# State products of units 1 to 3 in the accumulators' banks, and two loads of unit 1 moved

## The chip, the cores and the metric

The kernel runs on one core of one Trainium2 chip. A core has a matrix engine (TensorE, "PE" in the profile), a vector engine (VectorE, DVE), an engine for pointwise functions (ScalarE, ACT), a general-purpose engine (GpSimd, POOL) and an engine that only issues transfers (Sync, SP). They run side by side, each takes its own instructions in order, and they wait for each other through semaphores. Matrix results are written to PSUM[...]; everything else lies in SBUF. Transfers from and to the main memory (DMA) can be issued by Sync, ScalarE and GpSimd.

The metric is the device time of one execution in microseconds, lower is better. Before the change it is 333.74 us, the median of three executions (333.68 to 335.12).

## What is computed

The reference has two parts. The first is a chunked state-space scan over `x`, with decay `a` and the vectors `B` and `C`:

```
log_a = log(clip(a, 1e-6, 1));  state = 0
for each chunk of 32 positions:
    cum  = cumsum(log_a in the chunk)
    M    = (C B^T) * exp(cum_i - cum_j), for j <= i
    y    = M x + (C state) * exp(cum)
    state = exp(sum(log_a)) * state + sum_j exp(cum_last - cum_j) * B_j x_j
```

with batch 4, 8 heads, 768 positions, head size 32 and state size 16. The second part takes the 3072 rows of `y`, 256 wide, through two dense layers: `out = silu(y @ w_in) @ w_out`, with a middle width of 2048.

## The kernel before

The positions are cut into twelve units of 256 positions (`UT`), three to a batch entry (`UPB`), and each unit into four chunks of 64. Units 0, 1 and 2 are the first batch entry, unit 3 starts the second. Two units make a block of 512 rows for the dense layers; units 0 and 1, whose dense layers run first and piece by piece, are the "first pass", which the change lies in and just ahead of.

Nothing here is scheduled by a tool: each engine runs its instructions in the order in which the program text issues them. What sets the order are the calls at the end of the kernel (from line 696), then the strings of `steps` (line 835), then `PLAN` (line 849) for the later blocks.

One unit goes through these helpers, named in the profile by their lines:

- `load_n`, `load_t`, `load_x` (L125, L135, L143) load B, C and x. `load_n(u, 0, q)` loads B and `load_n(u, 1, q)` loads C with positions on the partitions, in two transfers each, on the queue `q`. One run of B or C is 16 floats, 64 bytes; one run of x is 32 floats.
- `f_P0` (L344) clamps `a` for the prefix products and `f_P` (L348) scans them on DVE.
- `f_Ab` (L363) spreads `a` over the partitions by a matmul into a bank of the pool `ps_a`; `f_Ek` (L356) scans it on DVE into the decay matrix E.
- `f_B` (L380) multiplies B by the last column of E, giving BT, on GpSimd for units 1 and 2.
- `f_TP` (L394) transposes B and C on PE for units 0 to 2, and ACT copies them out (L398, L401); `f_T2` (L408) makes the head-masked copies of C.
- `f_G` (L442) forms C B^T on PE, into columns 0 to 255 of the four banks of a tile `gy`.
- `f_D0` (L428) forms the state products, BT times x, on PE. Before the change they go to columns 256 to 383 of the first two banks of the same tile `gy`.
- `f_M` (L448) multiplies E in place by the result of `f_G`, on DVE, in two halves. `f_S` (L460, L462) runs the state recurrence over the four state products, on DVE. `f_SM` (L469) makes masked copies of the states on ACT. `f_C` (L412) multiplies C by the prefix products.
- `f_Y` (L482, L491) adds up the state part and the in-chunk part of y on PE into a new tile `gy`, and `f_X` (L501) copies it out on ACT as the dense layers' input.

PSUM is divided into `gy` (`ps_s`, one buffer of four banks), `hp` (`ps_h`, two buffers of one bank) and `a` (`ps_a`, two buffers of one bank). The last pair holds the output sums of the second dense layer, from the first call of `f_s2` on (L544, at 60 us); before that it holds the spread `a` of units 0 and 1.

The weights come as raw 64-bit numbers, in sixteen tiles of 128 x 4 KB (`raw 0` to `raw 15`, L183), and are turned into 32-bit floats on the chip: `w_size` takes two ACT instructions (L189 and L192), `w_bits` three on DVE (L203, L205, L206) and an addition on GpSimd or DVE (L208). The first dense layer of the first pass is `f_s1` (L531), two per unit and weight tile. Matmuls on a tile of zeros, `busy` (L298, L300), fill places where PE would stand still.

Around the change, in the order of the program: ACT does `w_size(0, "u")`, then `f_SM(0)`, later `w_size(2)`, `f_SM(1)`, `w_size(3, "u")`, `f_X(1)`. DVE does `f_M(1, 0)`, `f_P(1)`, `f_M(1, 1)`, `f_S(1)`. PE does `f_s1(0, 0)`, `f_G(1)`, `f_s1(0, 1)`, `f_D0(1)`, six matmuls of zeros, `f_Y(1)`, and then `f_s1(1, 0)`. Sync's queue issues, after the store of `a` for the first batch entry (L259): x of unit 1, raw 2, ab 2 (L113), pa 2 (L246), acl (L265), raw 3, C and B of unit 2, raw 4, x of unit 2. GpSimd, once its masks are made, issues B of unit 1, clamps `a` for unit 0, issues C of unit 1, and then runs `f_C(0)`.

Of the kernel before, what the change touches and what calls it, by code (L numbers as in the profile page):

```python
# [33 lines left out]
def kernel(  # L34
# [22 lines left out]
    nc = tc.nc  # L57
# [5 lines left out]
    UPB = S // UT  # L63
# [22 lines left out]
    def block(name, dtype=FP32):  # L86

        return blk.tile([128, 512], dtype, name=name, tag="blk", bufs=NB)
# [4 lines left out]
    def bank4(name="gy"):  # L93
        return ps_s.tile([128, 4, 512], FP32, name=name, tag="gy")

    def acc(name):
        return ps_a.tile([128, 512], FP32, name=name, tag="a")
# [3 lines left out]
    def at(u):  # L101
        return u // UPB, u % UPB * UT
# [13 lines left out]
    def load_n(u, i, q, ks=(0, 1)):  # L116
        b, t0 = at(u)
        if i == 1:
            if u not in tbc:
                tbc[u] = block("tbc0")[:, 0:256].rearrange("p (k h n) -> p k h n", k=2, h=H)  # L120
        elif u not in bn:
            bn[u] = (block("bn0")[:, 0:256].rearrange("p (k h n) -> p k h n", k=2, h=H) if u in (0, 1, 3) else
                     loads.tile([128, 2, H, N], FP32, name="bn"))
        for k in ks:
            q.dma_start(out=(bn, tbc)[i][u][:, k], in_=(B, C)[i][b, :, t0 + 128 * k:t0 + 128 * k + 128].rearrange("h p n -> p h n"))  # L125
# [12 lines left out]
    def load_x(u, q, ks=(0, 1)):  # L138
        b, t0 = at(u)
        if u not in xt:  # L140
            xt[u] = loads.tile([128, 2, H, D], FP32, name="xt", bufs=2)
        for k in ks:
            q.dma_start(out=xt[u][:, k], in_=x[b, :, t0 + 128 * k:t0 + 128 * k + 128].rearrange("h p d -> p h d"))  # L143
# [28 lines left out]
    def two(t):  # L172
        return t.rearrange("p (k f) -> p k f", k=2)
# [82 lines left out]
    def f_A():  # L256
        nc.vector.tensor_scalar(out=ach[A0:A1], in0=ach[A0:A1], scalar1=1.0, scalar2=1e-6, op0=ALU.min, op1=ALU.max)
        nc.vector.memset(ach[A0:A1, :, 0:1], 0.0)
        nc.sync.dma_start(out=a_first, in_=ach[A0:A1])  # L259
# [30 lines left out]
    def early(n):  # L290
        t = half("zero")
        for i in range(n):
            nc.tensor.matmul(out=t, lhsT=warm[:, 0:128], rhs=warm, start=True, stop=True)
# [24 lines left out]
    nc.scalar.activation(misc[:, 2 * UT - 1:], idle[:, 0:1], AF.Silu)  # L318
    early(6)
    f_A()  # L320
    load_x(1, nc.sync)
    hm = const.tile([128, H], FP32, name="hm")
    nc.gpsimd.memset(hm, 1.0)
# [17 lines left out]
    def f_P0(u, engine):  # L341
        src = pa[u].rearrange("p (c t) -> p c t", t=Q)
        PZ[u] = (pz, pz1, pz)[u]
        engine.tensor_scalar(out=PZ[u][:, :, 1:], in0=src, scalar1=1.0, scalar2=1e-6, op0=ALU.min, op1=ALU.max)  # L344
# [16 lines left out]
    def f_Ab(u, k, hs=slice(0, H), bank=acc):  # L361
        t = ab[u, k, hs.start] = bank("ab").rearrange("p (h t) -> p h t", t=Q)
        nc.tensor.matmul(out=t[:, hs].rearrange("p h t -> p (h t)"),  # L363
                         lhsT=sel[:A1, 2 * u + k].rearrange("r c m -> r (c m)"),
                         rhs=ach[:A1, hs].rearrange("r h t -> r (h t)"), start=True, stop=True)
# [49 lines left out]
    def new_dp(u):  # L415
        if u not in DP:
            DP[u] = bank4()
        return DP[u]

    def f_D0(u, ts=(0, 1, 2, 3)):  # L420
        last = u % UPB == UPB - 1
        bt = BT[u].rearrange("p k h n -> p k (h n)")
        xc = xt[u].rearrange("p k h d -> p k (h d)")
        d = [new_dp(u)[:, c, 256:384].rearrange("p (k x) -> p k x", k=2) for c in range(2)]
        for t in ts[:3 if last else 4]:
            k, c = divmod(t, 2)
            for g in range(4):
                nc.tensor.matmul(out=d[c][32 * g:32 * g + 32, k],  # L428
                                 lhsT=bt[64 * c:64 * c + 64, k, 32 * g:32 * g + 32],
                                 rhs=xc[64 * c:64 * c + 64, k, 64 * g:64 * g + 64], start=True, stop=True,  # L430
                                 tile_position=(64 * c, 32 * g), skip_group_check=True)
        BX[u] = d
        if 3 in ts:
            BT.pop(u)
# [258 lines left out]
                in_=r[32 * q:32 * q + 32].rearrange("p (b d) -> p b d", d=32))  # L693


    load_n(1, 0, nc.gpsimd)
    f_P0(0, nc.gpsimd)
    load_n(1, 1, nc.gpsimd)
    f_Ab(0, 0, slice(0, 4))
    f_Ab(0, 0, slice(4, 8))  # L700
    f_Ab(0, 1, slice(0, 4), half)
# [18 lines left out]
    f_Ek(0, 1, slice(4, 8))  # L720
    f_B(0)
    f_D0(0)
    f_Ab(1, 0)
    f_Ab(1, 1)
# [26 lines left out]
    f_G(1)  # L751
    f_s1(0, 1)
    f_D0(1)
    f_M(1, 0)
    f_P(1)
# [20 lines left out]
    def stage(u, what):  # L776
        for c in what:
# [16 lines left out]
            elif c == "P":  # L794
                f_P(u)
            elif c in "12":
                f_E1(u, int(c) - 1, 2)
            elif c == "B":
                f_B(u, nc.gpsimd if u == 2 else nc.vector)
            elif c == "C":  # L800
                f_C(u)
            elif c == "D":
                f_G(u)
                f_D0(u)
            elif c == "M":
                f_M(u, 0)
                f_M(u, 1)
            elif c == "S":
                f_S(u)
            elif c == "s":  # L810
                f_SM(u)
            elif c == "Y":
                f_Y(u)
                f_X(u)
            elif c == "h":
                f_xh(u)
            elif c == "l":
                f_xl(u)
            elif c == "d":
                f_xd(u)  # L820
# [137 lines left out]
```

## Time and profile before

| | us |
|---|---|
| median of three executions | 333.74 |
| the profiled execution | 336.35 |
| its span, first to last instruction | 334.3 |
| PE busy in the span | 325.1 (97%) |
| DVE busy | 250.8 (75%) |
| ACT busy | 220.9 (66%) |
| GpSimd busy | 78.3 (23%) |
| first pass ends, about (first L544) | 60 |

The profile is of one execution, whose time is 2.6 us above the median; its span leaves 2.05 us outside. The page cuts the span into 40 slices of 8.4 us and gives the busy share of each in tenths:

```profile
PE   8888999999999999999999999999999999999996
PEclk9897999999999999999999999999999999999999
DMA  6897895796883684164420164520263000012001
```

A 9 is 90% or more. PE has room in the first four slices only, 0 to 33 us, and in the second and fourth its granted clock (PEclk) is not full. A matmul's end in the profile is modelled, so a busy PE is not one at its peak; and an engine's idle time counts only where the end of the kernel waits for it. A line of the waits reads: engine and line that waited, what it waited for, total time, times, longest. A line of the timeline reads: start, length, engine, line, operation, output from input, count, and in brackets the idle time before it with what ended it.

### The profile page before, as it was taken

What the parts mean: (1) busy time and instruction counts of PE and PEld (TensorE: products, weight loads), DVE (VectorE), ACT (ScalarE), POOL (GpSimd) and SP (SyncE); (2) the same over time, 40 slices, a digit from 0 to 9 for tenths busy, and PEclk for the clock granted to TensorE, in tenths of its full rate; (3) what the DMA queues carried; (4) which work ended last, traced back from release to release, by engine and by line L of the source; (5) the groups of instructions that cost most, each with busy time, mean ns of one, the idle gap of its engine ahead of it and who ended that gap; (6) DMA issues with size and microseconds to landing.
All of it is one profiled execution on the core that took longest, in us unless ns stands there. A gap on an engine that the chain in (4) does not pass through costs nothing.

```text
span 334.3 us, 7996 instructions
## 1 busy us (share of the span) xinstructions
PE 325.1 (97%) x3229; PEld 262.9 (79%) x3229; DVE 250.8 (75%) x414; ACT 220.9 (66%) x422; POOL 78.3 (23%) x81
## 2 busy tenths in 40 slices
PE   8888999999999999999999999999999999999996
PEld 4456888888878778778778778778778778899996
DVE  7769787896887988997965996965996873494443
ACT  3443876976577898766666666767666756656662
POOL 8332313687111222231202231202230202000000
PEclk9897999999999999999999999999999999999999
DMA  6897895796883684164420164520263000012001
GB/s 129 227 187 194 215 286 202 181 197 126 153 164 68 114 156 80 47 112 77 96 54 0 47 112 87 108 33 0 52 108 65 2 2 0 0 23 43 2 0 63
DMA packets 90709, 31.87 MB, mean 95 GB/s; under 512 B 74433, under 2 KB 81345, under 8 KB 90673
## 3 DMA queue, kind: packets, MB, share of 16 engines
q1 hardware_dynamic: 85296, 25.47, 34.2%
q0 software_dynamic: 3008, 5.51, 9.2%
q10 hardware_dynamic: 2368, 0.39, 0.6%
q8 instruction: 25, 0.41, 0.5%
q14 instruction: 12, 0.09, 0.1%
HBM read 22.79 MB, written 3.32 MB: 78 GB/s over the span
## 4 chain that ended last, share of the span: by engine, by line
PE 95%; DMA 1%; SPq 1%; DVE 1%; issue 1%; ACT 0%; DVEq 0%
PE hp L567 23%; PE hp L559 11%; PE hp L531 9%; PE oa L608 9%; PE oa L609 9%; PE b L639 9%; PE oa L544 8%; PE gy L491 3%; PE b L634 2%; PE b L617 2%; PE oa L617 2%; PE gy L482 2%; PE gy L442 2%; PE gy L428 1%; DMA xt<-in_x_dram 1%
## 5 line engine op out<-in xcount | busy, mean ns | idle before, releaser
L561 ACT ACTIVATE hp<-hp 128x512 f32<-128x512 f32 x80 | 46.6, 582 | 72.5 <-PE hp L559 72.4
L581 DVE TENSOR_TENSOR gl<-g,gh 128x512 fp32r<-128x512 f32 x62 | 42.7, 689 | 50.7 <-ACT gh L577 47.6
L567 PE MATMUL hp<-xh,wh 128*128 128x512 f32 x160 | 65.5, 409 | 0.0
L585 DVE SCALAR_TENSOR_TENSOR gd<-gh,g 128x512 fp32r<-128x512 f32 x80 | 59.5, 747 | 5.2 <-ACT gh L577 5.2
L567 PE MATMUL hp<-xl,wl 128*128 128x512 f32 x160 | 62.8, 393 | 0.0
L581 POOL TENSOR_TENSOR gl<-g,gh 128x512 fp32r<-128x512 f32 x18 | 29.2, 1622 | 122.1 <-ACT gh L577 122.1
L577 ACT ACTIVATE gh<-g 128x512 fp32r<-128x512 f32 x80 | 50.5, 632 | 2.8
L608 PE MATMUL oa<-gh,wh 128*128 128x512 f32 x128 | 50.1, 391 | 0.0
L609 PE MATMUL oa<-gl,wl 128*128 128x512 f32 x128 | 50.0, 391 | 0.0
L559 PE MATMUL hp<-xd,wd 128*128 128x512 f32 x160 | 49.6, 391 | 0.0
L575 ACT ACTIVATE g<-hp 128x512 f32<-128x512 f32 x80 | 47.4, 593 | 0.6 <-PE hp L567 0.6
L567 PEld LDWEIGHTS hp<-xh,wh 128*128 128x128 f32 x160 | 30.1, 188 | 8.8 <-ACT hp L561 2.5
L559 PEld LDWEIGHTS hp<-xd,wd 128*128 128x128 f32 x160 | 30.0, 188 | 6.8
L639 PE MATMUL b<-gd,wd 128*128 128x512 f32 x128 | 34.6, 390 | 0.0
L567 PEld LDWEIGHTS hp<-xl,wl 128*128 128x128 f32 x160 | 30.1, 188 | 4.8
L531 PE MATMUL hp<-xf,w 128*128 128x256 f32 x128 | 31.7, 403 | 0.5 <-ACT xf L501 0.5
L356 DVE TENSOR_TENSOR_SCAN E<-ab,diag 128x512 f32<-128x512 f32 (+1 forms) x26 | 29.4, 1165 | 1.6 <-PE gy L491 1.0
L531 PEld LDWEIGHTS hp<-xf,w 128*128 128x128 f32 x128 | 25.2, 202 | 4.7 <-ACT xf L501 0.6
L544 PE MATMUL oa<-gT,w 128*128 128x256 f32 x128 | 28.4, 379 | 0.0
L608 PEld LDWEIGHTS oa<-gh,wh 128*128 128x128 f32 x128 | 24.0, 188 | 5.2
L639 PEld LDWEIGHTS b<-gd,wd 128*128 128x128 f32 x128 | 24.0, 188 | 5.1
L609 PEld LDWEIGHTS oa<-gl,wl 128*128 128x128 f32 x128 | 24.0, 188 | 5.1
(104 smaller groups left out, 463.2 us busy)
## 6 DMA issues: line engine op xcount, KB each, us to landing
ab<-a_zero SPq DMA_DIRECT2D x18, 256.0 KB
raw<-in_moe_w_in_dram SPq DMA_DIRECT2D x8, 512.0 KB
raw<-in_moe_w_out_dram SPq DMA_DIRECT2D x8, 512.0 KB
wl<-w POOLq DMA_DIRECT2D x16, 256.0 KB, 4.2
xt<-in_x_dram SPq DMA_DIRECT2D x24, 128.0 KB
out_dram<-ot SPq DMA_DIRECT2D x40, 64.0 KB
tbc<-in_C_dram SPq DMA_DIRECT2D x40, 32.0 KB
bn<-in_B_dram SPq DMA_DIRECT2D x20, 64.0 KB
```

Of the source, the lines that this page charges most:

```text
L531: nc.tensor.matmul(out=hp[:, i], lhsT=two(w32[j])[:, kc, 128 * i:128 * i + 128], rhs=two(XF[u])[:, kc], start=(kc == 0), stop=(kc == KC - 1))
L544: nc.tensor.matmul(out=OA[0][m][:, UT * u:UT * u + UT], lhsT=two(w32[8 + j])[:, i, 128 * m:128 * m + 128], rhs=two(GT[u, j])[:, i], start= ...
L559: nc.tensor.matmul(out=HP[s], lhsT=two(WD[f // 2])[:, kc, 128 * (f % 2):128 * (f % 2) + 128], rhs=XD[P][:, kc], start=(kc == 0), stop=Fals ...
L561: nc.scalar.activation(HP[s], HP[s], AF.Copy, scale=HALF / UP)
L567: nc.tensor.matmul(out=HP[s], lhsT=two(w[f // 2])[:, kc, 128 * (f % 2):128 * (f % 2) + 128], rhs=x_[P][:, kc], start=False, stop=(kc == KC ...
L575: nc.scalar.activation(G[s], HP.pop(s), AF.Silu, scale=UP)
L577: nc.scalar.activation(GH[s], G[s], AF.Copy, scale=DOWN)
L581: engine.tensor_tensor(out=GL[s], in0=G[s], in1=GH[s].bitcast(FP32), op=ALU.subtract)
L585: nc.vector.scalar_tensor_tensor(out=GD[s], in0=GH[s].bitcast(FP32), scalar=1.0 + 1.0 / HALF, in1=G.pop(s), op0=ALU.mult, op1=ALU.subtract)
L608: nc.tensor.matmul(out=OA[P][m], lhsT=two(WH[n])[:, r, ms], rhs=gh, start=(f == 0), stop=False)
L609: nc.tensor.matmul(out=OA[P][m], lhsT=two(WL[n])[:, r, ms], rhs=gl, start=False, stop=(f == NF - 1))
L639: nc.tensor.matmul(out=B2[P][:, m], lhsT=two(WD[n])[:, r, 128 * m:128 * m + 128], rhs=gd, start=(fresh and s == tiles[0]), stop=True, skip ...
```

## The change

Three things are changed. The state products of units 1, 2 and 3 go to two tiles of the pool `ps_a`, one bank each, in place of columns 256 to 383 of `gy`; those of unit 0 and of units 4 to 11 stay. The load of B of unit 1 is issued on GpSimd's queue behind the clamp of unit 0 in place of ahead of it. And the load of C of unit 1 is issued on Sync's queue, between the store of `a` and the load of x of unit 1, in place of on GpSimd's queue. One line is added near the top, so that lines after 320 count one more, and after `f_D0` four more.

```diff
     early(6)
     f_A()
+    load_n(1, 1, nc.sync)
     load_x(1, nc.sync)
     hm = const.tile([128, H], FP32, name="hm")
...
-        d = [new_dp(u)[:, c, 256:384].rearrange("p (k x) -> p k x", k=2) for c in range(2)]
+        if 0 < u <= UPB:
+            d = [two(acc("d")[:, 0:128]) for c in range(2)]
+        else:
+            d = [two(new_dp(u)[:, c, 256:384]) for c in range(2)]
         for t in ts[:3 if last else 4]:
             k, c = divmod(t, 2)
             for g in range(4):
...
+    f_P0(0, nc.gpsimd)
     load_n(1, 0, nc.gpsimd)
-    f_P0(0, nc.gpsimd)
-    load_n(1, 1, nc.gpsimd)
     f_Ab(0, 0, slice(0, 4))
```

`acc("d")` takes the next of the two buffers of `ps_a`, and `two` views 128 columns as 2 x 64.

## The prediction

> **What bounds the kernel now.** I read the summary, the chain that ended last, then the waits of the first 60 us engine by engine, and last a table of half-microsecond stretches. The summary gives TensorE (PE) 97% busy of a 334.3 us span, and the chain is 95% PE. After 28 us PE waits for nothing the profile shows up to 60 us, so an edit to units 1 to 3 can only pay in PE's idle time before 28 us, or where PE runs slowly. The waits of PE in the first 60 us (total, times, longest):
>
> ```profile
> PE gy L482 <- ACT sm L469: 2.4, 1, 2.4
> PE gy L482 <- issue: 1.6, 1, 1.6
> PE hp L531 <- ACT xf L501: 0.5, 1, 0.5
> ```
>
> L482 is the state part of f_Y, once per unit: 1.6 us is unit 0's, 2.4 us unit 1's. The chain through unit 1 (start, length):
>
> ```profile
> 21.84 0.49 PE gy L428 x32
> ...
> 22.46 0.69 DVE E L448
> 23.15 0.60 DVE pfx L348
> 23.75 0.58 DVE E L448
> ...
> 25.19 0.70 ACT sm L469 x2
> ...
> 25.98 0.69 PE gy L482 x32
> ...
> 27.94 5.40 PE hp L531 x16
> ```
>
> So VectorE (DVE) starts unit 1's multiply f_M (L448) only after the state products f_D0 (L428), and ScalarE (ACT) and PE follow in single file. The engine rows show how long DVE stood before it, and what held ACT in unit 0:
>
> ```profile
> 17.28 2.33 DVE L356 TENSOR_TENSOR_SCAN E<-ab,diag 128x512 f32<-128x512 f32 x2
> 22.46 0.69 DVE L448 TENSOR_TENSOR E<-gy,E 128x512 f32<-128x512 f32 x1 [2.85 <-PE gy L428]
> ...
> 19.74 0.64 POOL L380 TENSOR_TENSOR BT<-bn,E 128x256 f32<-128x256 f32 x1 [0.88 <-PE hp L531]
> ...
> 11.86 0.66 ACT L189 ACTIVATE wu<-raw 128x512 f32<-128x512 f32 x1 [5.01 <-DMA raw<-in_moe_w_in_dram]
> ```
>
> In unit 0, ACT's in-order queue has the weight conversion L189 ahead of f_SM (L469), so the landing of raw 0 at 11.86 sets f_Y's start at 13.14. The stretch table adds the clock (columns: stretch, length, busy time and instructions of PE, weight loads, DVE, ACT and GpSimd, then granted clock, DMA share, GB/s):
>
> ```profile
> 14.50:15.00 0.50, 0.50 (x3) 0.22 (x3) 0.50 (x2) 0.46 (x2) 0.37 (x1) 0.50 0.13 20
> ...
> 28.50:29.00 0.50, 0.50 (x3) 0.41 (x2) 0.50 (x2) 0.21 (x1) 0.00 (x0) 0.50 0.18 41
> ```
>
> The clock reads 0.50, half speed, from about 14.43 to 17.84 and from 28.08 to 31.49 (edges worked out from the partly slow half microseconds at 0.93, 0.66, 0.58 and 0.51). The second one falls on needed work: 16 L531 matmuls take 5.40 us from 27.94, where 8 take 1.73 at 33.78; 5.40 - 2 x 1.73 = 1.94 us lost.
>
> [...] f_M reads columns 0 to 255 of banks into whose columns 256 to 383 f_D0 writes, and DVE stood 2.85 us. [...] both slow stretches are 3.41 us and 13.65 us apart[...]. [...]
>
> **The change part by part.** Times are of the profiled execution (336.35 us, of which the span is 334.3); its sum is carried to the median 333.74.
>
> 1. State products of units 1 to 3 into the accumulator banks. f_M of unit 1 then needs f_G, which ends at 19.92, and, since it overwrites E, GpSimd's BT, which ends at 20.38; say 20.48 in place of 22.46. With the old spacings (0.61, 0.60, 0.58) the prefix scan is at 21.09, the second f_M at 21.69, f_S could be at 22.27. But f_S reads the products: they end at 22.33, plus the 0.13 seen before f_M, gives 22.46. Its third step frees f_SM 0.94 later, 23.40 (from 24.25 to 25.19 in the old chain). Now ACT is late: it converts raw 2 from 22.38 to 23.61, ahead of f_SM. So f_SM at 23.65 and, 0.79 later, f_Y at 24.44: 1.54 us earlier. The prefix scan is earlier too, so GpSimd's f_C (23.92, 0.68 long) moves before 23 us. The new tiles reuse the two banks that the decay scans read until 19.61, and BT has waited for these already: nothing. In units 2 and 3 f_S stands ahead of f_M on DVE, so nothing moves; there PE had no wait. The first accumulation needs the banks at 60.05, f_S of unit 3 ends at 52.76: nothing.
>
> 2. B of unit 1 behind the clamp on GpSimd. The clamp L344 waited for its own data until 6.10, so it doesn't move. B's two issues (2.04 us) take the place of C's (1.80, from 6.55), and f_C of unit 0 slips from 8.43 to about 8.65, ends at 9.33, and is needed after 11.5: nothing. Before raw 0 lands, the DMA engines lose C's GpSimd traffic: GpSimd's queue took 16.6% of 2 us, 40.2, 4.0, 13.6 and 27.0% of one from 6 to 12 us, 1.18 us of all sixteen, for B and most of C. About half, 0.5, goes. Raw 0 lands 0 to 0.6 earlier (a loss is excluded, since C now stands behind it in the queue, but for B's share at worst 0.2); I take 0.4. DVE runs almost without a gap from 13.64 to 19.61, so the 0.4 passes on to unit 1.
>
> 3. C of unit 1 on Sync, ahead of x. Two issues of about 0.6 (L125 on Sync at 18.54: 1.43 for two) and 2048 packets of 64 bytes. From 22 to 24 us the same kind shows 2244 packets at 79.4% of 2 us: 1.45 us of all sixteen engines for 2048. Everything later on that queue (x of unit 1, raw 2, ab 2, pa 2, acl, raw 3, C and B of unit 2, raw 4, x 2) lands later by 1.45 less C's and B's share on GpSimd: 0.5 to 1.5, I take 1.0. C itself takes the place that x 1 had, whose last packets ran to 15.2; the transposes L394 need it at 16.12 less 0.4: just covered. The queue stood blocked from 7.88 to 14.43 (issues of 3.66 and 2.85 us), so the extra issues lie in that. [...] Raw 2 flowed from 15.2 to 17.0; a microsecond later is still ahead of ACT's use at 22. Raw 3's packets of 2 KB were through by 22.0 (of the 2244 from 22 to 24 us, 11 are that large) and ACT took it at 25.79; it must now be converted before f_X of unit 1, so by 24.6: 23.0 fits.
>
> 4. The clock. PE's idle stretch was 23.63 to 25.98 and is now about 0.8 us. The window from 24.67 to 28.08 had 1.75 us idle and 1.5 of small tiled matmuls, and was followed by half speed; the one before had 1.06 idle and was not. The new one starts L531 at 27.94 - 1.94 = 26.0, so most of it is dense. I take the 1.94 us as regained; the ends are -0.3 (the slow window merely starts elsewhere, on busier work) and 1.94.
>
> 5. What is late next. PE then runs 3.9 us ahead of the old trace at 33 us, while transfers are 1.0 later. Sync's queue was busy 98% of 36 to 52 us, raw 5 was issued at 27.81 and converted at 36.46, raw 6 at 33.54 and 40.73: about 4 us of slack left for 4.9 to be taken. Two banks (hp) stand between ACT and PE. So I give back 0.9 (bounds 0 and 2).
>
> Sum: 1.54 + 0.4 + 1.94 - 0.9 = 2.98 less: 333.4 for the profiled run, and in proportion 333.74 - 2.95 = **330.8**.
>
> **Rivals.** (B) Only the waits shrink. The unprofiled runs are 2.6 us shorter than the profiled one, so half speed may not strike there, or the slow window moves on. Then 1.54 + 0.4 less 0.4 given back: 332.2. [...] against: the three runs agree but for one 1.4 longer. (C) The transfers are the real clock of 28 to 52 us (98% busy): what PE gains it waits for at raw 5 or raw 6; about 333.6. Against: PE and ACT had no DMA wait there. (D) The other side: C's small packets on the one in-order queue push raw 3 past its time. ACT takes raw 3 ahead of f_X, so PE waits microsecond for microsecond. It costs from a landing at 24.6, decides when it eats the 1.9 gained (26.5), and with 28.5 gives 335.8. For it: single issues there stood 3.2 us [...]; against: that needs four times the 1.45 us that C costs. That the change doesn't do what it says is no rival: the wait of f_M on f_D0's count goes out of the built program.
>
> **How the numbers follow.** Forecast 0.50 (its own range 329.2 to 331.8), B 0.27, C 0.12, D 0.11. About 0.5%, 1.67 us, is what a measurement of this kernel can tell from no change. Faster by more: all of the forecast and two thirds of B, 0.68; within: the rest of B, C and a little of D, 0.21; slower: 0.11. The range runs from 329.2 (everything regained, little given back) to 333.5, which leaves out D, half of C and a little below.
>
> **What would show it.** Right: f_M (L452 there) of unit 1 starts by 20.5 and no longer names f_D0; f_Y of unit 1 starts near 24; PE's wait for sm is under 1 us; L531 after it runs 16 matmuls in about 3.5 us at clock 1.00; raw 0 lands before 11.86. Wrong: ACT waits for a raw tile, the transposes wait for C, a half-speed window lies at 24 to 31 us all the same, or new PE waits appear between 33 and 60 us.

## The result, and the profile after

The changed kernel takes 332.64 us (median of 20 executions, 330.76 to 335.40), the kernel before, run beside it, 333.91 us (20 executions, 331.75 to 335.15). The ratio is 0.9967 with a 95% interval of [0.9944, 0.9989]: about 1.1 us less (the medians differ by 1.27). The sign is as forecast, but the forecast was 2.95 us less, so more than half of it is missing.

The profiled execution of the changed kernel took 330.76 us (span 329.0), 5.6 us less than the profiled one of before. That pair of profiles exaggerates the change, as the experiments show. The chain through unit 1 in the changed kernel's timeline (start, length; in brackets the idle time before and what ended it):

```profile
14.92 2.32 DVE L357 TENSOR_TENSOR_SCAN E<-ab,diag 128x512 f32<-128x512 f32 x2
18.04 0.69 DVE L452 TENSOR_TENSOR E<-gy,E 128x512 f32<-128x512 f32 x1 [0.80 <-POOL BT L381]
...
18.70 0.46 PE L432 MATMUL d<-xt,BT 64*32 64x64 f32 x32
...
20.84 0.69 ACT L473 ACTIVATE sm<-st,par 128x128 f32<-128x128 f32 x2 [0.30 <-DVE st L466]
...
21.64 0.69 PE L486 MATMUL gy<-cw,sm 32*64 32x64 f32 x32 [1.08 <-POOL pz L345]
...
23.59 3.72 PE L535 MATMUL hp<-xf,w 128*128 128x256 f32 x16 [0.47 <-ACT xf L505]
...
27.15 0.38 PE L395 MATMUL gy<-ident,bn 128*128 128x128 f32 x2
...
54.59 7.72 PE L548 MATMUL oa<-gT,w 128*128 128x256 f32 x35
```

f_M of unit 1 (L452) now starts ahead of the state products (L432) and waits for GpSimd's BT. From the start of the state products (21.77 in the timeline before) to f_Y (L486) it was 25.98 - 21.77 = 4.21 us and is 21.64 - 18.70 = 2.94. The sixteen matmuls of L535 take 3.72 us, not 5.40: no half speed (granted clock 1.00 from 20 to 26 us). Granted clock over the span, in tenths:

```profile
PEclk9999999999999999999999999999999999999999
```

And ACT's waits for raw tiles of the first weights in the first 60 us (total, times, longest), where the forecast had named the danger:

```profile
ACT wu L189 <- DMA raw<-in_moe_w_in_dram: 7.4, 5, 2.9
```

ACT waits for them five times, where before it did so once, for raw 0. PE's own waits in this profile name neither the weights nor gT (what ACT makes of the first layer's sums).

What follows the first L544 (L548 in the changed kernel) is nearly the same: 334.3 - 59.88 = 274.42 us before, 329.0 - 54.59 = 274.41 after, and 273.9 to 274.9 in all eighteen profiles. So nearly all of the differences below arise ahead of it.

### The profile page after: what moved, and what is told of

Same layout as the page of the kernel before. It is cut to its first block, busy times and chain, and to the rows that moved or that the text cites. A ratio compares the mean times of both kernels' runs of the same rounds, so it can differ in the third digit from the quotient of the medians.

```text
span 329.0 us, 7993 instructions
## 1 busy us (share of the span) xinstructions
PE 321.2 (98%) x3226; PEld 260.5 (79%) x3229; DVE 251.4 (76%) x414; ACT 220.7 (67%) x422; POOL 76.5 (23%) x79
## 3 DMA queue, kind: packets, MB, share of 16 engines
q0 software_dynamic: 2944, 5.38, 9.1%
## 4 chain that ended last, share of the span: by engine, by line
PE 87%; DMA 5%; DVE 4%; issue 2%; SPq 1%; POOL 1%; ACT 1%; DVEq 0%
PE hp L571 23%; PE hp L563 11%; PE oa L612 9%; PE oa L613 9%; PE b L643 9%; PE oa L548 8%; PE hp L535 3%; PE b L638 2%; PE b L621 2%; PE oa L621 2%; PE gy L495 2%; PE gy L446 2%; DMA bn<-in_B_dram 2%; DMA raw<-in_moe_w_in_dram 2%; PE gy L486 2%
## 5 line engine op out<-in xcount | busy, mean ns | idle before, releaser
L535 PE MATMUL hp<-xf,w 128*128 128x256 f32 x128 | 29.8, 385 | 0.6 <-ACT xf L505 0.5
L548 PE MATMUL oa<-gT,w 128*128 128x256 f32 x128 | 28.4, 379 | 0.0
L535 PEld LDWEIGHTS hp<-xf,w 128*128 128x128 f32 x128 | 23.6, 190 | 4.5 <-ACT xf L505 0.6
```

The lines of the kernel that those rows point to most:

```text
L535: nc.tensor.matmul(out=hp[:, i], lhsT=two(w32[j])[:, kc, 128 * i:128 * i + 128], rhs=two(XF[u])[:, kc], start=(kc == 0), stop=(kc == KC - 1))
L548: nc.tensor.matmul(out=OA[0][m][:, UT * u:UT * u + UT], lhsT=two(w32[8 + j])[:, i, 128 * m:128 * m + 128], rhs=two(GT[u, j])[:, i], start= ...
```

## The experiments

Each set compared its kernels with the kernel before on one chip, and the chips differ by up to 1 us, so numbers are compared within a set. "Full clock" counts the executions whose mean granted clock is 0.998 or more; the mean time of those alone stands beside it. A half-speed window is a stretch at clock 0.50, 3.41 us long in the profile of before; one of them in a span of 334 lowers the mean clock by 0.005 (3.41 x 0.5 / 334), and the windows of an execution are counted by that.

| set, kernel | ratio to before | 95% interval | full clock | mean of these, us |
|---|---|---|---|---|
| 1 before (75 executions) | | | 17 of 75 | 332.28 |
| 1 changed | 0.9984 | [0.9962, 1.0005] | 14 of 22 | 332.94 |
| 1 banks alone | 0.9961 | [0.9938, 0.9984] | 17 of 22 | 332.08 |
| 1 loads alone | 1.0012 | [0.9994, 1.0030] | 3 of 22 | 332.86 |
| 2 before (72) | | | 18 of 72 | 333.13 |
| 2 before, 16 zeros | 0.9972 | [0.9953, 0.9992] | 18 of 19 | 333.11 |
| 2 changed, 10 zeros | 0.9979 | [0.9960, 0.9999] | 19 of 22 | 333.39 |
| 2 before, half loads | 0.9996 | [0.9976, 1.0015] | 6 of 22 | 332.53 |
| 2 changed, half loads | 0.9954 | [0.9935, 0.9974] | 15 of 22 | 332.54 |
| 3 before (59) | | | 15 of 59 | 332.85 |
| 3 changed, raw 5, 6 ahead | 0.9985 | [0.9954, 1.0015] | 5 of 14 | 332.93 |
| 3 banks, raw 5, 6 ahead | 0.9975 | [0.9953, 0.9997] | 15 of 22 | 332.63 |
| 3 before, raw 5, 6 ahead | 1.0013 | [0.9983, 1.0043] | 1 of 14 | 332.84 |
| 3 before, 16 zeros, raw 5, 6 ahead | 0.9962 | [0.9941, 0.9983] | 20 of 22 | 332.61 |
| 4 before (60) | | | 14 of 60 | 332.56 |
| 4 changed, 10 zeros, half loads | 0.9947 | [0.9928, 0.9966] | 17 of 19 | 331.86 |
| 4 before, 16 zeros, half loads | 0.9963 | [0.9944, 0.9982] | 21 of 22 | 332.65 |
| 4 changed, 10 zeros, raw 5, 6, 7 ahead | 1.0083 | [1.0061, 1.0105] | 2 of 22 | 335.38 |
| 4 banks, 10 zeros, raw 5, 6, 7 ahead | 1.0061 | [1.0020, 1.0101] | 3 of 10 | 333.36 |

### Set 1: the parts

The kernel before again, and the changed one:

> The kernel before once more, nothing changed. Theory W (windows): the profiled execution of before was an unusual one, with two half-speed windows of the matrix clock; most executions have one or none. Then this profile has a mean clock of 0.995 or more, a time near 333.9 us, and the first L544 nearer 58 than 60 us. Theory T (transfers): the two windows are there in every execution and the gain of the change is lost later, while PE waits for raw tiles; then the clock is 0.990 again and the first L544 is at 60 us.

> The changed kernel once more, nothing changed. Theory W: 0.996 of before; where its executions have a mean clock of 0.995 they are about 2 us longer than where it is 0.998 or more. Theory T: the first L548 comes at 56 to 57 us in a profile whose time is at the median of 332.6, after 1.5 to 2 us of waits of PE between 28 and 55 us that the first profile of it did not have.

The move of the state products alone:

```diff
-        d = [new_dp(u)[:, c, 256:384].rearrange("p (k x) -> p k x", k=2) for c in range(2)]
+        if 0 < u <= UPB:
+            d = [two(acc("d")[:, 0:128]) for c in range(2)]
+        else:
+            d = [two(new_dp(u)[:, c, 256:384]) for c in range(2)]
```

> Only the state products of units 1 to 3 move to the accumulators' banks; the loads are those of before. By my prediction's step 1 f_Y of unit 1 starts 1.5 us earlier: 332.4, ratio 0.995. Theory W: between 0.994 and 0.999, as the wait goes in every execution. Theory T, and a rival by which the loads carry the whole gain: ratio 0.999 to 1.001.

The two loads alone:

```diff
     f_A()
+    load_n(1, 1, nc.sync)
     load_x(1, nc.sync)
...
+    f_P0(0, nc.gpsimd)
     load_n(1, 0, nc.gpsimd)
-    f_P0(0, nc.gpsimd)
-    load_n(1, 1, nc.gpsimd)
```

> Only the loads of B and C of unit 1 move; the state products stay in gy. By steps 2 and 3 raw 0 lands 0.4 us earlier and later transfers 1 us later: 333.5, ratio 0.999. The profile of the changed kernel showed raw 0 landing at 9.47 in place of 11.86; if that is due to the loads and is there in every execution, f_Y of unit 0 starts about 2 us earlier here, and the ratio is about 0.994 to 0.997.

The banks alone give the gain (0.9961, where the whole change has 0.9984); the loads alone give nothing (1.0012). The new profile of the kernel before has no late raw 0 in it: unit 0's f_Y starts at 11.59 us, without the 1.6 us gap. But f_Y of unit 1 waits and half speed follows, as in the first profile, here for 6.8 us, two windows in a row (clock 0.50 from about 23.8 to 30.7). Its mean clock is 0.988, near what T expected of every execution:

```profile
22.89 0.69 PE L482 MATMUL gy<-cw,sm 32*64 32x64 f32 x32 [2.35 <-ACT sm L469]
...
25.05 6.47 PE L531 MATMUL hp<-xf,w 128*128 128x256 f32 x16 [0.48 <-ACT xf L501]
31.36 0.38 PE L394 MATMUL gy<-ident,bn 128*128 128x128 f32 x2
...
58.06 4.26 PE L544 MATMUL oa<-gT,w 128*128 128x256 f32 x19
```

The changed kernel in the same set:

```profile
14.68 0.33 PE L395 MATMUL gy<-ident,tbc 128*128 128x128 f32 x1 [0.43 <-DMA tbc<-in_C_dram]
...
22.24 0.69 PE L486 MATMUL gy<-cw,sm 32*64 32x64 f32 x32 [1.07 <-POOL acl L273]
...
24.20 3.72 PE L535 MATMUL hp<-xf,w 128*128 128x256 f32 x16 [0.47 <-ACT xf L505]
27.75 0.38 PE L395 MATMUL gy<-ident,bn 128*128 128x128 f32 x2
...
45.23 1.99 PE L535 MATMUL hp<-xf,w 128*128 128x256 f32 x8 [1.43 <-ACT gT L538]
...
56.98 5.34 PE L548 MATMUL oa<-gT,w 128*128 128x256 f32 x24
```

At the second transposes (L394, here L395) the changed kernel is 31.36 - 27.75 = 3.61 us ahead: f_Y comes 0.65 earlier, and the two slow windows, which made PE's work after it (L491 and L531) 2.95 us longer, are not there. At the first L548 it is only 58.06 - 56.98 = 1.08 ahead. The rest goes in between: PE waits for gT 1.7 us in all, as T expected, and the page shows ACT behind it, waiting 7.9 us in five for raw tiles. And C of unit 1, now on Sync's queue, holds up the first transposes by 0.43.

That pair is not the typical one. The kernel before had full clock in 17 of 75 executions (mean 332.28), a mean clock near 0.995 in 31 (333.35) and of 0.990 or less in 27 (334.61): executions whose mean clock is lower by one half-speed window are about 1.1 us longer, by two about 2.3. The changed kernel at full clock (332.94) is not faster than the kernel before at full clock (standard errors 0.26 and 0.22). Two theories were left after this: that the change only removes half-speed windows (W), and that the raw tiles take back what the shorter wait gains (T).

### Set 2: fill the wait, and halve the loads

To have full clock with the wait left in, the zero matmuls ahead of f_Y of unit 1 were made sixteen in the kernel before, and ten in the changed one:

```diff
-    busy(6)
+    busy(16)
     f_Y(1)
```

> The kernel before with sixteen matmuls of zeros instead of six ahead of f_Y of unit 1, which fill the 2.4 us that PE stands there; nothing else is changed and the data wait stays. Theory W: the clock is full at 28 to 31 us in nearly all executions; the time is as good as with the change, 332.3 to 332.9, ratio 0.996 to 0.998. Theory T agrees on that, since what PE gains beyond some 1.3 us goes to waits for transfers. A rival theory P (the earlier f_M is what pays, the clock is a bystander): 333.6, ratio 1.000; if the zeros run over the end of the wait it is 0.2 to 0.5 slower.

> The changed kernel with ten matmuls of zeros instead of six ahead of f_Y of unit 1, filling the 1.07 us that PE still stands there. Theory W: the few executions with a slow stretch (6 of 20, 8 of 22) lose it; 332.3 to 332.7, 0.3 us less than the changed kernel. Theory T: at most 0.3 less, since the raw tiles set the pace. Theory P: no change.

The fill does for the kernel before what the change does: 0.9972, full clock in 18 of 19. f_Y still comes at its late time, but PE is busy till then, and the sixteen matmuls behind it take 3.72 us (mean clock of the profiled execution 1.000):

```profile
19.99 3.63 PE L298 MATMUL zero<-misc 128*128 128x512 bf16 x16
23.81 0.69 PE L482 MATMUL gy<-cw,sm 32*64 32x64 f32 x32 [0.19 <-ACT sm L469]
...
25.76 3.72 PE L531 MATMUL hp<-xf,w 128*128 128x256 f32 x16 [0.47 <-ACT xf L501]
...
56.09 6.21 PE L544 MATMUL oa<-gT,w 128*128 128x256 f32 x28
```

PE then has no wait for gT up to L544. At full clock the kernel before is at 333.13 without the fill and at 333.11 with it, so the fill gains time by the clock alone, as W has it; P falls. In the changed kernel ten zeros bring nothing beyond the change (0.9979), and the change brings no more than the fill.

For T, raw 5 to raw 8 were loaded by half and the rest set to zeros:

```diff
         t = raw[n] = quad.tile([128, 2, WF, 2], U32, name="raw", tag="quad")
+        if n in (5, 6, 7, 8):
+            nc.gpsimd.memset(t[:, :, WF // 2:].rearrange("p k f two -> p k (f two)").bitcast(FP32), 0.0)
+            q.dma_start(out=t[:, :, :WF // 2].rearrange("p k f two -> p k (f two)"), in_=src[:, :, :WF // 2].bitcast(U32))
+            return
```

> The kernel before, with only the first half of the columns of raw 5 to raw 8 loaded and the other half set to zeros by GpSimd: 1 MB less to transfer; half of the weights in tiles 5 to 8 is left out, the instructions on PE, DVE and ACT are the same. Theory T (the transfers from 28 to 52 us set the pace of the first pass, so the change hands its gain to waits for raw 5 to raw 8): the kernel before is held by PE's own slow stretch there and waited for raw tiles only 2.5 us on ACT, which cost PE little; it gains 0 to 0.8 us, ratio 0.998 to 1.000. Theory W (the change does nothing but remove slow-clock stretches that come in some executions, and the transfers are no limit): no gain, 1.000.

> The changed kernel with the same half loads of raw 5 to raw 8; half of the weights in tiles 5 to 8 is left out. Theory T: PE keeps the 3.6 us by which it was ahead at the second transposes; the waits of ACT for raw tiles (7.9 us) and of PE for gT (1.7 us) go; 330.3 to 331.3 us, ratio about 0.991 against the kernel before, 2 us or more less than the changed kernel (333.06). Theory W: as the changed kernel, 332.5 to 333.2, ratio 0.997 to 0.998.

The kernel before gains nothing (0.9996), the changed one comes to 0.9954, a smaller gain than T's 0.991. This did not decide: half-speed windows came and went, and the profiled execution of the changed kernel, with a mean clock of 0.990, as two windows give, took 6.41 us for the sixteen matmuls in place of 3.72:

```profile
25.30 6.41 PE L539 MATMUL hp<-xf,w 128*128 128x256 f32 x16 [1.33 <-ACT xf L509]
```

Here f_X itself was late, and PE waited 1.33 us for it in place of 0.47: ACT had stood 2.2 us for raw 3, which it converts ahead of f_X.

### Set 3: raw 5 and raw 6 earlier

While raw tiles are late, the DMA engines are not always busy. A table of 2 us stretches of the changed kernel in set 1 (last two columns: DMA share, GB/s) has these rows:

```profile
32.00:34.00 2.00, 2.00 (x11) 1.75 (x10) 1.68 (x5) 0.77 (x2) 0.98 (x1) 1.00 0.49 137
34.00:36.00 2.00, 1.75 (x9) 1.23 (x8) 1.97 (x5) 2.00 (x5) 0.49 (x1) 1.00 0.38 78
```

Sync was busy until 34.21 with the issues of B and C of unit 3 (L135, eight from 29.36 on), with raw 6 behind them. Theory Q: the order on Sync's queue is what gives back; V: the volume, in any order.

```diff
-    f_A3()
     load_w(5, nc.sync)
+    f_A3()
+    load_w(6, nc.sync)
     load_bcx(3, "c")
-    load_w(6, nc.sync)
```

It was put into the changed kernel, the banks alone, the kernel before, and the kernel before with sixteen zeros:

> The changed kernel with two loads moved on Sync's queue: raw 5 ahead of the three stores of the other batch entries' a, raw 6 ahead of B and C of unit 3; the same work and bytes. Theory Q (the give-back comes from Sync's queue standing blocked by small issues while the transfer engines are 40 to 50% busy from 28 to 30 and from 32 to 36 us, so an earlier issue lands raw 5 to raw 8 earlier): raw 5 and 6 are issued 4 to 5 us earlier, converted 3 us earlier, the gT waits of PE (1.7 us) go, 330.3 to 331.7 us on this scale where the changed kernel is at 332.6 to 333.1; ratio 0.992 to 0.995. Theory V (the volume until 52 us sets the pace, whatever its order): as the changed kernel, 0.996 to 0.998, ACT still waits 6 us or more for raw tiles.

> The move of the state products alone, with the same two loads of raw tiles moved ahead. Theory Q: as the changed kernel with that edit or up to 0.5 us better, since C of unit 1 stays off Sync's queue: ratio 0.991 to 0.995. Theory V: as the banks alone, 0.995 to 0.997.

> The kernel before with only the two loads of raw tiles moved ahead. PE is not held by raw tiles there (the half loads gained it nothing, 0.9996), so under Q and V alike no change: ratio 0.999 to 1.001. A gain of over 0.3% would say that transfers do bound the kernel before.

> The kernel before with sixteen matmuls of zeros instead of six ahead of f_Y of unit 1 and the two loads moved ahead: full clock, but the wait of f_M on the state products stays. Under Q the difference between this and the banks with the same loads is what the removed wait itself is worth once transfers give way: this one at 0.995 to 0.997 (nothing beyond the fill alone), 0.8 to 1.4 us slower than the banks. If the removed wait is worth nothing, the two are equal.

None gains clearly beyond its own version without the edit. Raw 5 and raw 6 do come earlier, but raw 7 does not. ACT's conversions and PE in the changed kernel with the edit:

```profile
35.50 0.67 ACT L189 ACTIVATE wu<-raw 128x512 f32<-128x512 f32 x1
...
43.84 0.67 ACT L189 ACTIVATE wu<-raw 128x512 f32<-128x512 f32 x1 [3.17 <-DMA raw<-in_moe_w_in_dram]
...
45.60 2.46 PE L535 MATMUL hp<-xf,w 128*128 128x256 f32 x8 [2.11 <-ACT gT L538]
```

Raw 6 is converted at 35.50 without a wait, where it was 37.74 after a wait of 1.71. Raw 7, issued at 37.30 behind the small loads of unit 3, is converted at 43.84, and PE's one wait for gT is 2.1 us. Slow matmuls follow that wait too (L446 takes 1.15 us in place of 0.69, L432 0.68 in place of 0.46; the mean clock of this execution is 0.995), and full clock is rarer than in the changed kernel without the edit (5 of 14, against 14 of 22 in set 1).

### Set 4: full clock throughout, and raw 7

The half loads once more, with ten and sixteen zeros, so that the clock is full in nearly all executions of both kernels:

> The changed kernel with ten matmuls of zeros ahead of f_Y of unit 1 (full clock in nearly all executions) and raw 5 to raw 8 loaded by half; half of the weights in tiles 5 to 8 is left out. Theory Q (landings of raw 5 to raw 8 take back what PE gains): no wait of PE for gT is left and ACT's waits for raw tiles fall under 5 us; first L552 at 54.4 to 55 us; 330.3 to 331.3 us, 1.5 us or more less than the fill alone (after with ten: 332.1 to 334 at full clock). Theory N (the spread between executions, not the transfers, is all there is): as the changed kernel, ratio 0.997 to 0.998.

> The kernel before with sixteen matmuls of zeros there and raw 5 to raw 8 loaded by half; half of the weights in tiles 5 to 8 is left out. With full clock PE had no wait for gT in it even with whole loads (first L544 at 56.1 us), so Q expects nothing more than the fill alone, ratio 0.996 to 0.997, and 1.2 to 1.6 us above the changed kernel with the half loads: that is what the removed wait is worth when transfers don't take it back. N: equal to it.

This decides for T in kind. At full clock the changed kernel is at 331.86 us (17 executions, standard error 0.14), the kernel before at 332.65 (21, 0.12): 0.79 us less, where with whole loads in set 2 the same pair stood at 333.39 and 333.11, 0.28 more (standard error 0.31). The removed wait is worth something once the raw tiles are not late. (The changed kernel here has its moved loads too; the banks alone were not run with half loads.) It is less than the 1.2 to 1.6 expected, and in the profile the next transfers are late. PE's timeline in the changed kernel with half loads (lines count four more):

```profile
38.04 7.17 PE L539 MATMUL hp<-xf,w 128*128 128x256 f32 x32
45.15 0.69 PE L450 MATMUL gy<-ce,bh 32*64 32x128 f32 x32
46.36 0.46 PE L436 MATMUL d<-xt,BT 64*32 64x64 f32 x32 [0.52 <-DVE BT L385]
```

and DVE's waits there:

```profile
DVE pfx L353 <- DMA pz<-a_in: 2.5, 1, 2.5
DVE E L361 <- DMA ab<-a_zero: 1.4, 1, 1.4
```

The 32 matmuls run through without a wait for gT, but unit 3's decays are waited for, and BT of unit 3 comes 0.5 us late.

Last, with ten zeros and set 3's edit, raw 7 was taken ahead of B and C of unit 3 as well:

```diff
     load_w(6, nc.sync)
+    load_w(7, nc.sync)
     load_bcx(3, "c")
...
-(1, 1, "2:TB a3 s4 2:a r7")
+(1, 1, "2:TB a3 s4 2:a")
```

> The changed kernel with ten matmuls of zeros, raw 5 ahead of the stores of a, and raw 6 and raw 7 ahead of B and C of unit 3 on Sync's queue. With raw 5 and 6 moved alone, raw 7 was still issued at 37.3 us and converted at 43.84, and PE waited 2.1 us for gT there. Q: raw 7 is issued by 31, converted by 39, no wait for gT of over 0.3 us; 330.5 to 331.5, ratio 0.991 to 0.994. The risk: B, C and decays of unit 3 come 2 us later, and DVE or PE waits for them at 36 to 45 us; then no gain, 0.997. V (the volume until 52 us decides): no gain, and ACT waits for raw 8 or the decays for ab in place of raw 7.

> The move of the state products alone, with the same ten matmuls and the same three raw loads ahead. Q: as the run before or up to 0.5 us better, since C of unit 1 stays off Sync's queue; ratio 0.990 to 0.994. V: 0.996 to 0.997.

Raw 7 is converted at 40.74 without a wait in the first of them, and no wait for gT is left in either; yet both are slower, 1.0083 and 1.0061, slower than any of the theories expected. Q falls; the risk that its expectation named came, and larger: the loss goes to what was pushed back. PE's timeline in the changed kernel with this edit, and then DVE's waits:

```profile
48.23 0.46 PE L432 MATMUL d<-xt,BT 64*32 64x64 f32 x32 [2.35 <-DVE BT L381]
48.62 5.38 PE L535 MATMUL hp<-xf,w 128*128 128x256 f32 x16
```

```profile
DVE bh L386 <- DMA tbc<-in_B_dram: 2.8, 1, 2.8
...
DVE E L357 <- DMA ab<-a_zero: 2.3, 1, 2.3
```

B and decays of unit 3 are late, PE waits 2.35 us for BT, and slow matmuls follow that wait: the sixteen behind it take 5.38 us in place of 3.72 (mean clock 0.993), and full clock is rare (2 of 22). The banks with this edit show the same (a wait of 2.73, then 5.37; mean clock 0.994).

No version that does the whole work is better than the change beyond the uncertainty of the ratios. The banks alone (0.9961), or the kernel before with sixteen zeros and raw 5 and raw 6 ahead (0.9962), are as good.

## Why the prediction was half right

- **Step 1, the banks: right in kind, short in size.** f_M of unit 1 no longer waits for the state products, for which it stood 2.85 us before, though it reads other columns of those banks (why, no run shows). But it waits 0.80 for BT and starts 0.66 ahead of them (18.04 and 18.70), not 1.29 (20.48 and 21.77). Measured from their start, f_Y came 1.27 us earlier in both pairs of profiles of the two kernels (4.21 to 2.94 in the first; 22.89 - 18.68 and 22.24 - 19.31 in set 1), against 1.54 forecast, and 0.6 to 1.2 earlier in the eight other profiles with the products moved. PE's wait there fell from 2.35 to 1.07 in these two pairs. ACT's masked states are late next, as forecast, but they wait 0.30 for DVE's states, not for the conversion of raw 2; they end at 20.84 + 0.69 = 21.53, just ahead of f_Y at 21.64 (the page names GpSimd's pz for that wait).
- **Step 2, B behind the clamp: not shown.** From 8 to 9 us Sync's queue took 83.1% and GpSimd's 40.2% of the time of the 16 DMA engines; that the one slowed the other was the author's estimate. In set 1 unit 0's f_Y starts at 11.59 in both kernels, and the loads alone gain nothing. The gap of 1.61 us that the 0.4 was taken from is the largest of any profile; gaps of 0.85 and 0.77 came again in versions of the kernel before, and one of 0.71 with the loads moved.
- **Step 3, C on Sync's queue: the cover was too thin.** The transposes waited 0.43 us for C in set 1 and 0.48 for B in the first profile. In set 1 the state products of unit 1 start at 19.31, against 18.68 in the kernel before: 0.63 of step 1's 1.27 is gone at once. In sets 2 to 4 the transposes of the changed kernel wait 0.3 or less, and the products are not later than in the kernel before. At full clock the banks alone are 0.86 us below the whole change (332.08 and 332.94, standard errors 0.23 and 0.26), in set 1 only. Rival D's mechanism did come, in a small size: ACT waits 0.2 to 2.2 us for raw 3 in every profile with the products moved, and where that was 1.4 to 2.2 f_X was late and PE waited 0.82 to 1.33 for it in place of 0.47. It came with the banks alone too, so C's packets are not its only cause.
- **Step 4, the clock: right in kind, wrong in size.** The slow windows after f_Y do come from PE's wait: with the place filled they are gone in 18 of 19 executions. How much idling sets half speed off was the author's estimate, from one stretch of each kind, and is not shown: in the first profile PE was idle for 1.79 us of the 3.41 ahead of the slow stretch (24.67 to 28.08). The 1.94 us were read too high, since sixteen of these matmuls take 3.72 at full clock: 5.40 - 3.72 = 1.68. And they were taken as lost in every execution. Over the four sets 64 of 266 executions of the kernel before had full clock, and 103 a mean clock under 0.992. In set 1 a window, counted by the mean clock, went with about 1.1 us of the kernel's time; why it is less than 1.68 is not shown. In that set an execution had (31 + 2 x 27) / 75 = 1.13 windows before and (7 + 2 x 1) / 22 = 0.41 with the change: 0.72 fewer, an estimate of 0.8 us in place of 1.94. That lies between the two measurements of the change, 0.5 us in set 1 and 1.1 in the first comparison (16 of 20 executions at full clock).
- **Step 5, the give-back: the step that failed most.** 0.9 was taken, with bounds of 0 and 2. From the second transposes to the first L548 the change lost 3.61 - 1.08 = 2.53 us in set 1, and the banks alone 2.97. The forecast had read 4 us of slack for raw 5 and raw 6; that slack was measured in a trace in which PE ran late, from two slow windows and a late raw 0. PE can indeed come about 3.9 us earlier than in that trace at hardly any loss: in the kernel before with sixteen zeros it reaches the second transposes at 29.32, not 33.18, and takes 56.09 - 29.32 = 26.77 us from there, where the profiles in which PE comes later take 26.70. But set 1's profile of the kernel before is at 31.36, so by these numbers only about 2 us of slack are left to it (an estimate across two chips), and the change came to 27.75, 3.6 ahead. What it gains beyond the slack is waited for again, and at full clock the change is not faster than the kernel before in sets 1 and 2. Rival C, the transfers as the real clock of 28 to 52 us, named this mechanism; together with rival B's doubt about the clock it describes the result better than the forecast's sum. Three of the forecast's own signs of being wrong were there: ACT waits for raw tiles, in set 1 the transposes wait for C, and in set 1 PE waits anew between 33 and 60 us.

The loss is not the same in every execution: in the first profile of the changed kernel PE passed the second transposes at 27.15 and lost only 54.59 - 27.15 - 26.70 = 0.74. There raw 5 to raw 7 were converted 1.2 to 2.1 us earlier than in set 1; why is open. How much of the loss belongs to each small load of unit 3 was not separated either.

## What to carry to other kernels

A profile is one execution. Before a stall or a slow-clock stretch in it is priced, compare its time with the other executions': here it was 2.6 us above the median, and two of the terms of the sum were partly its own. And slack of transfers read in a late execution is slack against lateness; when a wait in front of a phase that the transfers feed is removed, price the phase's feed at the pace that the change would set. If a gain is one of clock alone, filling the idle place with matmuls of zeros can bring it, as it did here (0.9972, the change itself 0.9967 and 0.9984).

## What the runs showed of the hardware

- Half speed came in some executions of the same program and not in others: 24% of the executions of the kernel before had a mean clock of 0.998 or more, on four chips (17 of 75, 18 of 72, 15 of 59, 14 of 60). After the wait of 2.35 us on PE ahead of small tiled matmuls it lasted 3.4 us in the first profile (5.40 for the sixteen matmuls behind it) and 6.8 in set 1's (6.47). With that place filled 1 of 19 executions was below 0.998 (set 2). Of the changed kernel, whose wait was 1.08 and 1.07 us in its two profiles, 12 of 42 were. Waits of 2.11, 2.35 and 2.73 us at other places, between 43 and 49 us, were followed by slow matmuls too (sets 3 and 4: 1.15 us for L446 in place of 0.69, and 5.38 and 5.37 for sixteen in place of 3.72).
- In the changed kernel the loads of B and C of unit 3 stood ahead of raw 6 on Sync's queue: eight issues of 32 KB each (L135) took 4.8 us of it in set 1, with the DMA engines at 0.49 and 0.38 of their time from 32 to 36 us, and raw 6 was converted at 37.74, after a wait of 1.71. With raw 6 ahead of them it was converted at 35.50 without a wait (set 3). How much of the 4.8 us is waiting was not separated. To put raw 5 and raw 6 first gained nothing here (0.9985, where the change without it has 0.9984).
